# Batch 0 of attention and a maxout network in one kernel: scores before denominators, the first k transposed while q comes, and a new order of loads

## The chip, the cores and the metric

The kernel runs on one core of a Trainium2 chip. The metric is the device time of one execution in microseconds. The engines are named as in the profile: PE (TensorE, the matrix multiplications), DVE (VectorE), ACT (ScalarE), POOL (GpSimd) and SP (SyncE). DMAs are issued by SP, POOL and, twice at the start, by ACT.

## The reference

Eight batches, twelve heads, 448 positions, 64 values per head. Attention with one added to the softmax's denominator, then a maxout network with three first weights and one output weight:

```python
scores = scale * np.matmul(q, k.transpose(0, 1, 3, 2))
m = np.max(scores, axis=-1, keepdims=True)
e = np.exp(scores - m)
attn = e / (np.sum(e, axis=-1, keepdims=True) + np.exp(-m) + 1e-09)
x = np.matmul(attn, v)         # heads side by side: (3584, 768)
h = np.maximum(np.maximum(x @ w1, x @ w2), x @ w3)
out = h @ w_out                # all four weights are 768 x 768
```

The inputs and the output are float32; the kernel multiplies in float16. It leaves the maximum out: exp(s) / (sum of exp(s) + 1) is the same quotient.

## The kernel before

**Tiling.** Two heads make a pair, so a batch has six pairs (`NPAIR`), and pairs are numbered 0 to 47 through all batches. The 448 positions are held as three chunks of 128 and one of 64 (`NB` = 3, `SL` = 64); position 7p + c of a batch stands on partition p in one half of the raw tile. A score tile has keys on partitions and 448 queries along the row, two heads side by side; `scores(p, c)` makes chunk c of pair p, `scores_last(p)` the short chunk of both heads in one matmul. `exp_scores` and `exp_last` are ACT's exponentials. A softmax denominator is a matmul of the exponentials with ones (`den`), the numerator one with v scaled by 256 (`av`, `vst`). ACT computes 1/den as exp(-ln(den + 1)) (`log_one`, `exp_one`), and DVE multiplies it into `xT`, the transposed input of the network (`normalize_one`). In batch 0 denominator and numerator are separate tiles; from batch 1 on one tile holds both (`av_main`, `reciprocals`, `normalize`).

**Loads.** `load(p0, n_pairs, names)` issues, for each of q, k and v, one DMA for the upper and one for the lower half of the partitions, on SP in general. `load_v` does the same for v alone on POOL, and `load_weight(i, half)` loads weight i (0 to 2 are w1 to w3, 3 is w_out), with the cast to float16 done by the DMA, on POOL. There are four sets of raw tiles, each for two pairs (pairs 0 and 1, 2 and 3, and so on, in turn). Pairs of odd batches want zeros in some rows of q, which DVE writes with a memset before the load of the lower half; that DMA waits for it.

**Transposes.** q and k are cast to float16 (`cast_q`, `cast_k`, `cast_k_last`; `cast_qk` does all) and, for pairs 0 to 11 (`P_DMA` = 12), transposed by PE: eight 128 x 128 transposes into one tile in PSUM, which DVE copies to `qkT`. For pair 0 the copy is split between DVE and ACT (lines 243 and 244). From pair 12 on a DMA transposes them. The PSUM pools have two buffers each: `ps_s` for scores, `ps_av` for denominators and numerators, `ps_u` for everything else, the transposes among it, unless `in_scores` puts them into `ps_s`.

**Order.** The order of the instructions of each engine is that of the program, written out by hand (`manual_schedule`). `keep_busy(n)` puts n matmuls of zeros on PE. The loop over `it` from 0 to 11 handles pair `it`:

- `it` 0 makes the scores of pair 0 and the first ones of pair 1. `it` 1 to 4 make the rest of the scores of pair `it`, the denominators and numerators of the pair before, and the transposes and first scores of the pair after.
- `it` 5 ends batch 0: it finishes pairs 4 and 5, transposes pair 6, and starts the network on batch 0 with three tiles of the first weight (`up`), the first four of whose six contraction chunks need pairs 0 to 3 only.
- `batch_done(b)` then puts the rest of that batch's network into a queue, 18 `up` groups of six matmuls (six for each of w1, w2, w3) and six or eight `op` groups (the output weight, 384 columns each). `group()` takes one from the queue. `it` 6 to 11 take three groups each between the steps of attention; the first `op` group comes in `it` 11.
- After the loop, pairs 12 to 47 go two at a time through a second loop, which takes eight to ten groups in each round and ends with what is left in the queue.

**What orders the loads.** SP and POOL issue strictly in program order, and an issue that waits holds up all behind it. SP's loads at `it` 3, 5 and 6 stand behind the memsets of line 498, and POOL's weights behind the scalings of v (`scale_v`), since these are on POOL too. The first half of weight 0 waits in addition for a memset of one column (line 535), which serves as a gate. The weights 1, 2 and 3 follow at `it` 5, 6 and 8; POOL reaches them at 24.71, 26.63 and 30.24 us, as it is far ahead of PE.

Of the kernel before, what the change touches and what calls it, by code (L numbers as in the profile page):

```python
# [21 lines left out]
def kernel(  # L22
# [83 lines left out]
    def load_v(p0, n_pairs):  # L106
        load(p0, n_pairs, "v", (nc.gpsimd, nc.gpsimd))
# [51 lines left out]
        )  # L159

    def cast_qk(p):
        if p == 0:

            qt, kt, _ = raw[0]
            nc.scalar.copy(
                out=k16[0][:, 0:NB], in_=kt[:, 0:2, 0:NB].rearrange("p h c d -> p c h d")
            )
            for eng, cs in ((nc.scalar.copy, slice(0, 2)), (nc.vector.tensor_copy, slice(2, NB + 1))):
                eng(out=q16[0][:, cs], in_=qt[:, 0:2, cs].rearrange("p h c d -> p c h d"))
            cast_k_last(0, nc.gpsimd)  # L170
        else:
            cast_q(p)
            cast_k(p)

    def cast_q(p):
        qt = raw[(p // HB) % NRAW][0]
# [8 lines left out]
        else:  # L185
            nc.vector.tensor_copy(out=q6, in_=qt[:, hs].rearrange("p h c d -> p c h d"))  # L186

    def cast_k(p):
        kt = raw[(p // HB) % NRAW][1]
        hs = slice(2 * (p % HB), 2 * (p % HB) + 2)  # L190
        nc.vector.tensor_copy(  # L191
            out=k16[p % NK][:, 0:NB], in_=kt[:, hs, 0:NB].rearrange("p h c d -> p c h d")
        )
        cast_k_last(p, nc.vector)

    def cast_k_last(p, eng):
        kt = raw[(p // HB) % NRAW][1]
# [16 lines left out]
    def transposes(p, in_scores=False):  # L214
        odd = (p // NPAIR) % 2
        qkT = att_pool.tile([2 * D, 1024], MMDT, tag="qkT", bufs=3)
        qkTs[p] = qkT, 0, S
        if p >= P_DMA:
            nc.sync.dma_start_transpose(
                out=qkT.rearrange("q (c p) -> q c p", p=128),  # L220
                in_=qk16[p % NK].rearrange("p c h d -> p (c h d)"),
            )
            qkTs[p] = qkT, 64 * odd, 512
            return
        if in_scores:
            trT = ps_s.tile([128, 2, 1024], MMDT, tag="s", name="trT")[:, 0]
        else:
            trT = ps_u.tile([128, 1024], MMDT, tag="u", name="trT")


        order = (NB, 0, 1, 2) if odd else (0, 1, 2, NB)
        n0 = 0
        for c in order:
            nc.tensor.transpose(
                out=trT[:, n0 : n0 + 128], in_=q16[p % NK][:, c], identity=ident16
            )
            n0 += SL if c == NB else 128
        for c in range(NB + 1):
            nc.tensor.transpose(
                out=trT[:, S + c * 128 : S + c * 128 + 128], in_=k16[p % NK][:, c], identity=ident16  # L240
            )
        if p == 0:
            nc.vector.tensor_copy(out=qkT[:, 0 : S + 128], in_=trT[:, 0 : S + 128])
            nc.scalar.copy(out=qkT[:, S + 128 : S + 512], in_=trT[:, S + 128 : S + 512])
        else:
            nc.vector.tensor_copy(out=qkT[:, 0 : S + 512], in_=trT[:, 0 : S + 512])  # L246

    def scores(p, c):
        qkT, q0, k0 = qkTs[p]
# [226 lines left out]
    def group():  # L476
        if queue:
            queue.pop(0)()

    LEFT = 4  # L480
    waiting = None
    keep_busy(13)
    cast_qk(0)
    load_v(0, 1)
    transposes(0)
    keep_busy(3)
    for it in range(P_DMA):
# [3 lines left out]
        n_groups = -(-max(len(queue) - LEFT, 0) // to_next) if it % NPAIR else 4  # L491
        n_groups = max(3, min(5, n_groups))

        if it in (3, 5, 6):
            p_new = {3: 7, 5: 8, 6: 9}[it]
            n = p_new // HB % NRAW
            hs = slice(2 * (p_new % HB), 2 * (p_new % HB) + 2)
            nc.vector.memset(raw[n][0][64:128, hs, NB - 1 : NB + 1, :], 0.0)
            if it == 3:
                load(NPAIR, 2, "v")  # L500
                load(p_new, 1, "qk")
            else:
                load(p_new, 1)
        if it == 4:
            load_weight(0, 1)
        if it in (5, 6, 8):
            load_weight((5, 6, 8).index(it) + 1)
        if it < NPAIR:


            if it == 0:
                cast_qk(1)
                scale_v(0)
                load_v(1, 1)
                load_v(2, 2)
                exp_scores(0, 0, scores(0, 0))
                exp_scores(0, 1, scores(0, 1))
                keep_busy(2)
                exp_scores(0, 2, scores(0, 2))
                transposes(1)  # L520
                exp_last(0, scores_last(0))
                keep_busy(2)
                exp_scores(1, 0, scores(1, 0))
            else:
                last = it == NPAIR - 1
                if last:
                    normalize_one(*waiting)
                else:
                    cast_qk(it + 1)
                scale_v(it)  # L530
                if it == 1:
                    load_v(4, 2)
                if it == 3:

                    nc.vector.memset(w_sb[0][:, 0, 0:1], 0.0)
                    load_weight(0, 0)
                if waiting is not None and not last:
                    normalize_one(*waiting)
                exp_scores(p, 1, scores(p, 1))
                den, av = (ps_av.tile([128, 512], FP32, tag="av", name=n) for n in ("den", "av"))  # L540
                sums_main(prev, den, 1)
                stp = scores(p, 2)
                if not last:
                    transposes(it + 1)
                stl = scores_last(p)
                sums_last(prev, den, 1)
                exp_scores(p, 2, stp)
                exp_last(p, stl)
                lnd = log_one(den)
                if not last:  # L550
                    exp_scores(it + 1, 0, scores(it + 1, 0))
                    waiting = prev, av, exp_one(lnd)
                sums_main(prev, av, 0)
                sums_last(prev, av, 0)
            if it == NPAIR - 1:


                den5 = ps_s.tile([128, 2, 512], FP32, tag="s", name="den5")[:, 0]
                sums_main(p, den5, 1)
                sums_last(p, den5, 1)  # L560
                lnd5 = log_one(den5)
                av5 = ps_av.tile([128, 512], FP32, tag="av", name="av")
                sums_main(p, av5, 0)
                sums_last(p, av5, 0)
                rb, rb5 = exp_one(lnd), exp_one(lnd5)
                cast_qk(it + 1)
                normalize_one(prev, av, rb)
                normalize_one(p, av5, rb5)

                ups = [up_open(), up_open(), up_open(ps_av, "av")]  # L570
                for fc, ps in enumerate(ups):
                    up_part(ps, 0, 0, fc, range(4))
                transposes(it + 1, in_scores=True)
                for dc in (4, 5):
                    for fc, ps in enumerate(ups):
                        up_part(ps, 0, 0, fc, (dc,))
                        if dc == 5:
                            up_close(ps, 0, 0, fc)
                batch_done(0)
                del queue[0:3]  # L580
        elif it == NPAIR:
            exp_scores(p, 0, scores(p, 0))
            exp_scores(p, 1, scores(p, 1))
            group()
            cast_qk(it + 1)
            scale_v(it)
            exp_scores(p, 2, scores(p, 2))
            exp_last(p, scores_last(p))
            group()
            transposes(it + 1)  # L590
            group()
        else:
            late = it + 1 < P_DMA
            if not late:

                cast_qk(it + 2)
                transposes(it + 2)
                scale_v(it + 1)
                load(it + 5, 2)
            for c in range(2):  # L600
                exp_scores(p, c, scores(p, c))
            group()
            if late:
                cast_qk(it + 1)
            scale_v(it)
            avs = [av_main(prev, hh) for hh in range(2)]
            av_last(prev, avs)
            stp = scores(p, 2)
            stl = scores_last(p)
            rb = reciprocals(prev, avs)  # L610
            exp_scores(p, 2, stp)
            exp_last(p, stl)
            if late:
                transposes(it + 1)
            group()
            normalize(prev, 0, avs, rb)
            group()
            normalize(prev, 1, avs, rb)
            if it + 2 == P_DMA:
                cast_qk(it + 2)  # L620
                transposes(it + 2)
            for _ in range(n_groups - 3):
                group()
# [7 lines left out]

    avs = [av_main(P_DMA - 1, hh) for hh in range(2)]
    for p in range(P_DMA, NP, 2):
        more = p + 2 < NP
        left = max(len(queue) - LEFT, 0)
# [84 lines left out]
```

## Time and profile before

| | us |
|---|---|
| median of 3 runs | 364.43 (363.88 to 364.97) |
| the profiled execution | 364.45 |
| its span | 362.7 |
| PE busy | 352.6 (97%) |
| DVE, ACT, POOL busy | 244.6, 219.0, 59.1 |
| first scores on PE | 7.34 |
| first `up` on PE | 31.48 |
| first `op` on PE | 68.70 |
| last load of the first 16 pairs issued | 64.77 |

The chain that ended last is 82% PE and 12% DMA, and all of its DMA parts lie in front: loads of v, the first weight, q and k. The DMA engines are over nine tenths busy in nearly all of the slices up to 72 us. A page's busy time counts a matmul from its start to its modelled end, and neighbours overlap, so PE's share is no measure of how much is left; the times between starts are.

### The profile page before, as it was taken

Reading aid. Unit: us, or ns where it says so; the run is one execution under the profiler, and the core shown is the slowest. Engines: PE = TensorE matmul, PEld = TensorE weight load, DVE = VectorE, ACT = ScalarE, POOL = GpSimd, SP = SyncE. Lnnn points to the kernel's source line nnn. Section 1 sums busy time; section 2 is a strip of 40 time slices with the busy share of each in tenths; the row PEclk is TensorE's granted clock in tenths of the full one; section 3 lists DMA queues with packets and bytes.
Section 4 is the critical chain, followed back from the end, with each engine's and each line's share of the span. In section 5 each row is a group of like instructions: output and inputs, shape, how many; then the busy total and the mean of one; then the engine's idle time right before and its main releaser. Section 6 shows DMA issues by size and latency. Waiting matters only on the chain.

```text
span 362.7 us, 5892 instructions
## 1 busy us (share of the span) xinstructions
PE 352.6 (97%) x2072; PEld 165.8 (46%) x2072; DVE 244.6 (67%) x524; ACT 219.0 (60%) x317; POOL 59.1 (16%) x167
## 2 busy tenths in 40 slices
PE   8999998999999999999999999999999999999994
PEld 3334443444444444454444544444444544445552
DVE  4665676866768767767768768668658768646553
ACT  4994576666566765776676666667565767660000
POOL 5673011312011211111021121121121121000000
PEclk9999999999999999999999999999999999999999
DMA  6999999899583994689483995678665961104006
GB/s 174 229 232 238 219 234 242 176 218 247 114 182 89 299 208 105 136 190 228 112 193 71 259 226 112 153 171 232 149 150 78 234 195 29 29 13 120 0 2 174
DMA packets 84942, 58.59 MB, mean 162 GB/s; under 512 B 41680, under 2 KB 81136, under 8 KB 84912
## 3 DMA queue, kind: packets, MB, share of 16 engines
q1 hardware_dynamic: 80144, 51.79, 60.5%
q0 software_dynamic: 4400, 6.10, 9.1%
q10 hardware_dynamic: 368, 0.33, 0.4%
q8 instruction: 16, 0.26, 0.3%
q14 instruction: 14, 0.11, 0.1%
HBM read 42.47 MB, written 11.01 MB: 147 GB/s over the span
## 4 chain that ended last, share of the span: by engine, by line
PE 82%; DMA 12%; POOL 2%; DVE 2%; issue 1%; ACT 0%; POOLq 0%; DVEq 0%
PE up L389 43%; PE op L423 14%; PE av L303 12%; PE stp L252 7%; DMA kin<-in_k_dram 4%; PE av L315 3%; DMA w<-in_moe_w_dram 3%; DMA vin<-in_v_dram 3%; PE stl L282 2%; DMA qin<-in_q_dram 2%; DVE o_sb L448 1%; POOL vin L92 1%; DVE hT L403 0%; DVE xT L337 0%; POOL vst L157 0%
## 5 line engine op out<-in xcount | busy, mean ns | idle before, releaser
L389 PE MATMUL up<-xT,w 128*128 128x448 f16 x864 | 175.2, 353 | 0.9 <-DMA w<-in_moe_w_dram 0.4
L262 ACT ACTIVATE eT<-stp 128x896 f16<-128x896 f32 x144 | 124.4, 911 | 24.5 <-PE stp L252 24.3
L389 PEld LDWEIGHTS <-w 128*128 128x128 f16 x864 | 80.4, 98 | 87.6 <-issue 17.0
L405 DVE TENSOR_TENSOR hT<-hT,up 128x448 f16<-128x448 f16 x96 | 59.1, 621 | 44.2 <-PE up L389 43.5
L157 POOL TENSOR_SCALAR vst<-vin 128x384 f16<-128x384 f32 x132 | 43.6, 341 | 246.9 <-PE av L303 135.6
L328 ACT ACTIVATE lnd<-av 64x448 f32<-64x448 f32 x84 | 45.2, 538 | 62.5 <-PE av L315 61.5
L423 PE MATMUL op<-w,hT 128*128 128x384 f16 x336 | 59.2, 326 | 0.0
L303 PE MATMUL av<-eT,vst 128*128 128x448 f16 x252 | 54.7, 352 | 0.6 <-DVE xT L337 0.6
L337 DVE TENSOR_TENSOR xT<-av,rb 64x448 f16<-64x448 f32 x84 | 52.0, 619 | 1.7
L403 DVE CAST hT<-up 128x448 f16<-128x448 f32 x48 | 29.1, 621 | 25.2 <-PE up L389 24.7
L448 DVE TENSOR_SCALAR o_sb<-op 128x384 f32<-128x384 f32 (+1 forms) x56 | 30.3, 551 | 21.0 <-PE op L423 20.2
L423 PEld LDWEIGHTS <-hT 128*128 128x128 f16 x336 | 31.4, 98 | 26.3 <-issue 5.3
L252 PE MATMUL stp<-qkT 64*128 64x448 f16 x288 | 41.4, 352 | 1.8 <-DVE qkT L246 1.4
L303 PEld LDWEIGHTS <-vst 128*128 128x128 f16 x252 | 24.6, 98 | 23.4 <-DVE xT L337 1.0
L191 DVE CAST qk<-kin 128x384 f16<-128x384 f32 x47 | 25.7, 547 | 2.3 <-DMA kin<-in_k_dram 2.1
L292 ACT ACTIVATE eL<-stl 128x896 f16<-128x896 f32 x18 | 16.5, 917 | 14.2 <-PE stl L282 14.2
L329 ACT ACTIVATE rb<-lnd 128x448 f32<-128x448 f32 x42 | 24.2, 576 | 1.4
L252 PEld LDWEIGHTS <-qkT 64*128 64x128 f16 x288 | 12.6, 94 | 20.1 <-issue 11.9
L199 DVE CAST qk<-kin 64x64 f16<-64x64 f32 x94 | 20.7, 221 | 1.2
L452 ACT ACTIVATE o_sb<-op 128x192 f32<-128x192 f32 x1 | 0.3, 331 | 31.3 <-DVE o_sb L448 31.3
L315 PE MATMUL av<-eL,vst 64*128 64x448 f16 x84 | 15.2, 360 | 0.0
L186 DVE CAST qk<-qin 128x512 f16<-128x512 f32 x29 | 13.2, 455 | 0.2
(54 smaller groups left out, 126.5 us busy)
## 6 DMA issues: line engine op xcount, KB each, us to landing
out_dram<-o_sb SPq DMA_DIRECT2D x54, 192.0 KB, 3.9
qin<-in_q_dram SPq DMA_DIRECT2D x20, 256.0 KB, 3.7
vin<-in_v_dram SPq DMA_DIRECT2D x20, 256.0 KB, 5.3
kin<-in_k_dram SPq DMA_DIRECT2D x19, 256.0 KB, 4.6
qin<-in_q_dram SPq DMA_DIRECT2D x20, 192.0 KB, 3.8
vin<-in_v_dram SPq DMA_DIRECT2D x20, 192.0 KB, 5.3
kin<-in_k_dram SPq DMA_DIRECT2D x19, 192.0 KB, 4.8
w<-in_moe_w_dram POOLq DMA_DIRECT2D x2, 1152.0 KB, 20.1
```

Source lines behind the costliest of these rows:

```text
L157: nc.gpsimd.tensor_scalar(out=out, in0=in_, scalar1=LAMBDA, scalar2=1.0, op0=ALU.mult, op1=ALU.mult)
L252: nc.tensor.matmul(out=stp[:, hh, 0:S], lhsT=qkT[hh * D : hh * D + D, k0 + c * 128 : k0 + c * 128 + 128], rhs=qkT[hh * D : hh * D + D, q0 ...
L262: nc.scalar.activation(out=eT[:, p % 3, c], in_=stp[:, :, 0:S], func=AF.Exp, scale=scale)
L303: nc.tensor.matmul(out=av[:, 0:S], lhsT=vst[:, p % VB, hh * NB + c, (1 - hh) * D : (3 - hh) * D], rhs=eT[:, p % 3, c, hh, :], start=(c == ...
L315: nc.tensor.matmul(out=avs[hh][:, 0:S], lhsT=vst[half, p % VB, 2 * NB, (1 - hh) * D : (3 - hh) * D], rhs=eL[half, p % 2, :], start=False, ...
L328: nc.scalar.activation(out=lnd[mine], in_=avs[hh][other, 0:S], func=AF.Ln, bias=1.0)
L337: nc.vector.tensor_tensor(out=xTs[b][mine, j, :], in0=avs[hh][mine, 0:S], in1=rb[mine], op=ALU.mult)
L389: nc.tensor.matmul(out=ps[:, 0:S], lhsT=w_sb[i][:, dc, ts(fc, 128)], rhs=xTs[b][:, dc, :], start=(dc == 0), stop=(dc == NDC - 1),)
L403: nc.vector.tensor_copy(out=h, in_=ps[:, 0:S])
L405: nc.vector.tensor_tensor(out=h, in0=h, in1=ps[:, 0:S], op=ALU.max)
L423: nc.tensor.matmul(out=ps[:, 0:NW], lhsT=hTs[sb][:, fc, ts(t, 128)], rhs=wout_sb[:, fc, ts(nh, NW)], start=(fc == 0), stop=(fc == NFC - 1),)
L448: nc.vector.tensor_scalar(out=o_sb[:, cs], in0=src, scalar1=1.0 / LAMBDA, scalar2=None, op0=ALU.mult)
```

## The change

- **Pair 0.** k is cast, transposed and copied first, into a score buffer; two zero matmuls follow; then q is cast, transposed into a second tile and copied. Both copies are DVE's, ACT's share of the copy is gone. Ahead of it `keep_busy(13)` becomes `keep_busy(8)`.
- **Pair 1.** The last rows of k are cast by POOL instead of DVE.
- **`it` 1 to 5.** Chunk 2's scores move in front of the denominators of the pair before; the short chunk's exponential is issued directly behind its matmul.
- **End of batch 0.** ACT's ln and exp for the last two pairs are interleaved.
- **v.** Pairs 2 and 3 get a load of their own each (pair 3's at `it` 1) instead of one for both.
- **Pairs 6, 7, 8.** v of pairs 6 and 7 and q and k of pair 7 move from `it` 3 to `it` 4, pair 8 from the start of `it` 5 to behind the normalization of pair 5, each with its memset (now `cleared(p)`). Pair 9 stays at `it` 6.
- **w_out.** It moves from `it` 8 to `it` 9, and waits for a memset of one column there.
- **Pair 7** is transposed in a score buffer.
- **Pair 11.** One group from the queue stands between its two numerators.

```diff
     def cast_qk(p):
-        if p == 0:
-            ...
-        else:
-            cast_q(p)
-            cast_k(p)
+        cast_q(p)
+        cast_k(p, nc.gpsimd if p == 1 else nc.vector)
+    def cast_k0():
+        nc.scalar.copy(
+            out=k16[0][:, 0:NB], in_=raw[0][1][:, 0:2, 0:NB].rearrange("p h c d -> p c h d")
+        )
+        cast_k_last(0, nc.gpsimd)
+    def cast_q0():
+        for eng, cs in ((nc.scalar.copy, slice(0, 2)), (nc.vector.tensor_copy, slice(2, NB + 1))):
+            eng(out=q16[0][:, cs], in_=raw[0][0][:, 0:2, cs].rearrange("p h c d -> p c h d"))
...
+        if p == 0:
+            trK = ps_s.tile([128, 2, 1024], MMDT, tag="s", name="trT")[:, 0]
+            for c in range(NB + 1):
+                nc.tensor.transpose(out=trK[:, ts(c, 128)], in_=k16[0][:, c], identity=ident16)
+            nc.vector.tensor_copy(out=qkT[:, S : S + 512], in_=trK[:, 0:512])
+            keep_busy(2)
+            cast_q0()
+            trQ = ps_u.tile([128, 1024], MMDT, tag="u", name="trT")
+            for c in range(NB + 1):
+                nc.tensor.transpose(out=trQ[:, ts(c, 128)], in_=q16[0][:, c], identity=ident16)
+            nc.vector.tensor_copy(out=qkT[:, 0:S], in_=trQ[:, 0:S])
+            return
...
+    def cleared(p):
+        hs = slice(2 * (p % HB), 2 * (p % HB) + 2)
+        nc.vector.memset(raw[p // HB % NRAW][0][64:128, hs, NB - 1 : NB + 1, :], 0.0)
...
-    keep_busy(13)
-    cast_qk(0)
+    keep_busy(8)
+    cast_k0()
     load_v(0, 1)
     transposes(0)
...
-        if it in (3, 5, 6):
-            ...
-            if it == 3:
+        if it in (4, 6):
+            cleared(7 if it == 4 else 9)
+            if it == 4:
                 load(NPAIR, 2, "v")
-                load(p_new, 1, "qk")
+                load(7, 1, "qk")
             else:
-                load(p_new, 1)
+                load(9, 1)
         if it == 4:
             load_weight(0, 1)
-        if it in (5, 6, 8):
-            load_weight((5, 6, 8).index(it) + 1)
+        if it in (5, 6):
+            load_weight(it - 4)
+        if it == 9:
+            nc.vector.memset(wout_sb[:, 0, 0:1], 0.0)
+            load_weight(3)
...
                 load_v(1, 1)
-                load_v(2, 2)
+                load_v(2, 1)
...
                 if it == 1:
+                    load_v(3, 1)
                     load_v(4, 2)
...
-                exp_scores(p, 1, scores(p, 1))
+                for c in (1, 2):
+                    exp_scores(p, c, scores(p, c))
                 den, av = (ps_av.tile([128, 512], FP32, tag="av", name=n) for n in ("den", "av"))
                 sums_main(prev, den, 1)
-                stp = scores(p, 2)
                 if not last:
                     transposes(it + 1)
-                stl = scores_last(p)
+                exp_last(p, scores_last(p))
                 sums_last(prev, den, 1)
-                exp_scores(p, 2, stp)
-                exp_last(p, stl)
                 lnd = log_one(den)
...
-                lnd5 = log_one(den5)
+                rb = exp_one(lnd)
+                rb5 = exp_one(log_one(den5))
                 ...
-                rb, rb5 = exp_one(lnd), exp_one(lnd5)
                 cast_qk(it + 1)
                 normalize_one(prev, av, rb)
                 normalize_one(p, av5, rb5)
+                cleared(8)
+                load(8, 1)
...
-            transposes(it + 1)
+            transposes(it + 1, in_scores=True)
...
-    avs = [av_main(P_DMA - 1, hh) for hh in range(2)]
+    avs = [av_main(P_DMA - 1, 0)]
+    group()
+    avs.append(av_main(P_DMA - 1, 1))
```

## The prediction

> **What bounds the kernel now.** I read the page first, then stretches of the span, then PE's waits, the places in PE's timeline where they stand, and last the DMA queues. After 90 us PE is all there is; before that it stands still here and there, and the DMA engines are full:
>
> ```profile
> PE 352.6 (97%) x2072; PEld 165.8 (46%) x2072; DVE 244.6 (67%) x524; ACT 219.0 (60%) x317; POOL 59.1 (16%) x167
> ...
> 31.00:60.00 29.00, 27.19 (x176) 12.69 (x175) 18.87 (x41) 17.43 (x27) 2.01 (x7) 1.00 1.15 233
> 60.00:90.00 30.00, 29.40 (x176) 13.37 (x174) 22.24 (x48) 19.12 (x29) 6.27 (x20) 1.00 0.93 217
> 90.00:340.00 250.00, 249.89 (x1434) 118.72 (x1433) 175.62 (x370) 157.16 (x224) 30.30 (x95) 1.00 0.63 148
> ```
>
> From 90 to 340 us PE is busy 249.89 of 250 with code that the change leaves alone, so whatever is won or lost before about 82 us is handed unchanged to the end. From 31 to 60 us the DMA share is 1.15: reordering loads only moves waits about unless it fills a stall. PE's waits between 31 and 90 us, and their places:
>
> ```profile
> PE trT L239 <- DVE qk L191: 1.0, 1, 1.0
> PE av L303 <- DVE xT L337: 0.6, 1, 0.6
> PE up L389 <- DMA w<-in_moe_w_dram: 0.4, 2, 0.2
> PE up L389 <- DVE hT L403: 0.3, 1, 0.3
> ...
> 36.20 1.31 PE L389 MATMUL up<-xT,w 128*128 128x448 f16 x6 [0.21 <-DMA w<-in_moe_w_dram]
> 41.95 1.31 PE L389 MATMUL up<-xT,w 128*128 128x448 f16 x6 [0.18 <-DMA w<-in_moe_w_dram]
> 59.11 0.54 PE L239 MATMUL trT<-ident,qk 128*128 128x128 f16 x4 [1.00 <-DVE qk L191]
> 68.70 1.15 PE L423 MATMUL op<-w,hT 128*128 128x384 f16 x6
> 75.20 0.74 PE L303 MATMUL av<-eT,vst 128*128 128x448 f16 x3 [0.57 <-DVE xT L337]
> ```
>
> "Idle" understates a stall, since the last matmul before it is drawn to its end. By starts: four transposes from 57.73 take 0.22 us, the next stand at 59.11 and come 0.1 us late themselves, so pair 10 lost 1.3 us; three numerator matmuls from 73.90 take 0.57, the next stand at 75.20, so 0.7 us went there. The chain of waits says what PE waits for: the first half of w1, then pair 10's k:
>
> ```profile
> 19.92 11.51 DMA w<-in_moe_w_dram
> 31.48 2.44 PE up L389 x12
> ...
> 43.03 15.35 DMA kin<-in_k_dram
> ```
>
> Three stretches give the DMA prices: 22 to 24.4 us (first pair of lines), 44 to 54 us, 58 to 68 us:
>
> ```profile
> q1 hardware_dynamic: 667, 0.56, 110.9%
> q0 software_dynamic: 3, 0.01, 1.4%
> ...
> q0 software_dynamic: 1000, 1.51, 82.5%
> q1 hardware_dynamic: 1004, 0.81, 31.7%
> ...
> q1 hardware_dynamic: 2784, 2.34, 111.2%
> ```
>
> q0 is POOL's queue, q1 SP's. Both full, they take turns packet by packet: 100 per us each. Alone, SP moves 278 per us, and POOL's full weights 141 (422 packets from 37.5 to 40.5 us). A full weight has 768 packets and 16 for its semaphore: 7.8 us shared, 5.6 alone. The weight issued at 19.92 has no data moving before 24.4: 4.5 us to start.
>
> **The change, part by part.**
>
> *Front.* k is transposed while q is on its way, so four transposes instead of eight follow q's cast at 5.98 us, and the copy behind them has 448 columns instead of 576 (0.46 us; 960 take 0.66, so 0.5 ns each and 0.39). First scores come 0.3 us sooner than 7.34. DVE copies k's half (0.43) before q lands at 5.5, unless that copy is late, which costs its overrun. If the spacing of 0.37 us in the first fillers (13 in 5.03 us) lasts longer now that they are eight, and two after k's transposes, the 0.3 becomes up to -0.4. Pair 1's last k rows move from DVE (0.62 us) to POOL (0.52), in POOL's wait for v (3.00 us idle before 8.74). None of this reaches the end: PE would arrive at its first `up` at 30.9 instead of 31.2, and the weight is not there.
>
> *Two score chunks ahead of the denominators.* Same matmuls between the same ends: the loop from one pair's first scores to the next (17.36, 21.30, 25.23: 3.93 us) is PE's work plus transposes, 0.66 us of copy, first scores. ACT loses a wait of some 0.17 us on chunk 2, but PE's loop doesn't shorten. 0, at most 4 x 0.17 us, and hidden likewise.
>
> *First weight half.* POOL issues it behind pair 3's scaling (19.92). Pair 3's v now has a load of its own, issued in iteration 1 where pairs 4 and 5 were issued (14.71); those needed 7.6 us for 256 KB, and half as much should land at 20 to 20.7. Then 1.0 us of scaling, so issue at 21.0 to 21.8 and data from about 26. SP loses little: pairs 6 and 7's v waits for nothing and goes out at 17.93 as before, only pair 7's second half of q and its k wait for the memset, about 21 instead of 17.4. But pair 8's memset is now behind batch 0's last normalization, at 31.9 instead of 25.28, so SP goes dry near 30 and the weight finishes alone: landing 31.3 against 31.43. Gain 0.15, bounds -0.3 and +0.6. Behind SP's wait stand pair 8's k and v and loads 9 and 10: at the shared rate pair 8's k lands near 38 and pair 9's near 46, cast after 43.8 and 50.2; that cover is four us each.
>
> *Second half and w2.* The second half lands alone near 34 (36.2 before): its wait of 0.3 us goes, and transposing pair 7 in a score buffer takes away the 0.5 us at 39.5. Both only carry PE to the next thing that is late, w2 (issued 24.71, 17.2 us to landing: 41.91). SP's stream is back with data at 33.9, and from there w2 shares: some 45 packets per engine at 16/100 us = 7.2 us, so 41.2 and 0.4 of receipt: 41.6. Gain so far 0.3; bounds 0 and 1.4 (all that PE could have gained).
>
> *Pair 10's k.* After w3 (some 49 us) nothing is in POOL's queue, SP runs alone, and pair 10's k lands near 53 instead of 58.38, five us before its transposes. Gain 1.3.
>
> *w_out.* Before, it was issued at 30.24 and landed 10 us ahead of its first use (68.70). Now POOL issues it behind a DVE memset that follows pair 7's second normalization in iteration 8 (55.57 before). From there to the first `op` are 13.1 us, 11.8 without pair 10's stall. The load needs about 0.1 for the memset, S to start, 7.8 us beside pairs 14 and 15 (still going: SP needs until 60 for load 12, alone), and 0.7 of receipt (issued 30.24 + 27.7 = 57.9; q0 is empty from 57.2). S lies between 2.5 (a v load issued at 9.73 landed whole 3.0 us later) and 4.5 (the weight above). The second is a weight on a full DMA, as here: S = 4.3, in all 12.9, a new wait of 1.1 us; bounds 0 and 1.6. It stands behind nothing else; av of pair 10 and three `op` groups wait behind it. POOL's scaling of pair 9, queued behind the gate, ends near 57.5 and is wanted after 62.
>
> By the Trainium skill, "DMA: Bandwidth & Descriptors", section "Latency and other measured facts", a POOL-issued DMA has its first byte after about 1 us. That would make 9.6 us and no wait; the row at 24.4 speaks against it.
>
> *An `op` group between pair 11's two numerators.* It takes 0.98 us and covers the 0.7 lost at 74.3. But there are two `op` groups left instead of three to hide pair 11's normalization, which ended at 80.06: the first `up` of batch 1 reaches its sixth k chunk some 0.6 us before that. Net +0.3; bounds -0.2 and +0.7.
>
> *Sum*, against the profiled execution's 364.45 us (its span 362.7 and 1.75 around it; the median of the runs is 364.43): 0.3 + 1.3 - 1.1 + 0.3 = 0.8 less, rounded up to 0.9 for ends of S that lie below: 363.5.
>
> **The rivals.**
>
> *No w_out wait.* If data starts within 3.2 us of the issue (4.3 less the wait), all of pair 10's 1.3 stays: 0.3 + 1.3 + 0.3 = 1.9 less, 362.5; with the bound of 1.4 at w2, 361.5. For it: the v load's 3.0 in all. Against: the start at 24.4. The skill's 1 us is this case.
>
> *Slower: the first weight waits for pair 3's v.* Were that load to land as late as pairs 4 and 5's in the profile (23.5), the weight would be issued at 24.6, start at 29.1, run alone for 3 us and land at 32.7. The second half follows at 35.7, w2 then shares from its first packet: 35.7 + 7.8 = 43.5, 1.6 later than 41.91. With the rest of the sum: -1.6 + 1.3 - 1.1 + 0.3 = 1.1 slower, 365.6. It decides once the weight is issued after about 23 us. For it: POOL stands strictly in order, and its queue did take 7.6 us here. Against: half the bytes.
>
> *The loads don't move what PE sees.* SP still issues v of pairs 6 and 7 where it did, and a DMA at 1.15 has as much to move. If pair 10's k stays late because pair 8 and 9's loads are issued 6 us later, its 1.3 us remains and the w_out wait falls away with it; only small gains are left, 364.3.
>
> **How the numbers follow.** Forecast 0.45, no w_out wait 0.33, slower 0.12, nothing moved 0.10. A measurement of this kernel can tell about 0.3% (1.1 us) from no change. Faster than that: the second case, and a third of the first where the wait is under 0.8: 0.47. Slower: most of the third case and a corner of the first: 0.11. Same: 0.42. Range: 361.9 (no wait and some gain at w2) to 364.9 (w_out at its worst, first weight a little late). The likeliest case alone: 362.9 to 364.2.
>
> **What would show it.** In PE's waits the entry of `trT` on `qk` (1.0) gone; `up` on `w` still there, once or twice, at 31 and 41 us; a new entry of `op` on the w_out load near 67 to 68 us; `av` on `xT` replaced by `up` on `xT` near 78 us. In POOL's timeline the first weight between 21.0 and 21.8, w_out near 55.4, landing 12 to 13 us later. In SP's timeline a hole from about 24 to 32 us. I am wrong if `op` doesn't wait, if the first `up` starts after 32 us, or if anything differs in length beyond 90 us.

## The result: slower by 0.7%, and the profile after

The changed kernel takes 367.26 us (median of 15 runs, 364.37 to 368.70); before, beside it, 364.52 us (15 runs, 363.88 to 365.57). The ratio is 1.007, 95% interval [1.0052, 1.0088]: slower by 2.7 us where 0.9 us faster was forecast, and outside the range. The profiled execution took 366.41 us (span 364.6), 1.96 more than the one of before. One execution of e2 (374.84 us, the one that its profile shows) and one of e3 (715.92 us) were slow, and all medians and ratios below leave them out.

Stretches of the span, after; the third column group is PE, and PEclk, DMA share and GB/s end the line:

```profile
31.00:60.00 29.00, 28.74 (x189) 13.58 (x187) 20.55 (x45) 17.46 (x27) 4.10 (x12) 1.00 1.15 234
60.00:90.00 30.00, 26.46 (x150) 12.20 (x149) 19.22 (x43) 17.63 (x27) 4.74 (x15) 0.94 0.88 200
90.00:340.00 250.00, 249.89 (x1434) 118.48 (x1433) 176.09 (x371) 158.28 (x225) 30.82 (x96) 1.00 0.65 151
```

Up to 60 us PE does more than before (28.74 us busy, 27.19 before), and beyond 90 us nothing has changed. All that is lost is lost between 60 and 90 us, and there are two losses in that line: PE is 2.9 us less busy, and its mean granted clock is 0.94, where before showed 1.00. PE's waits and the places in PE's timeline, after:

```profile
PE op L433 <- DMA w<-in_moe_w_out_dram: 2.8, 1, 2.8
PE up L399 <- DVE xT L347: 0.5, 1, 0.5
PE av L313 <- DVE xT L347: 0.2, 1, 0.2
PE up L399 <- DMA w<-in_moe_w_dram: 0.2, 1, 0.2
```

```profile
31.16 2.43 PE L399 MATMUL up<-xT,w 128*128 128x448 f16 x12
41.01 1.31 PE L399 MATMUL up<-xT,w 128*128 128x448 f16 x6 [0.17 <-DMA w<-in_moe_w_dram]
57.01 0.39 PE L253 MATMUL trT<-ident,qk 128*128 128x128 f16 x4
65.95 0.55 PE L262 MATMUL stp<-qkT 64*128 64x448 f16 x4
69.35 2.10 PE L433 MATMUL op<-w,hT 128*128 128x384 f16 x6 [2.85 <-DMA w<-in_moe_w_out_dram]
71.24 1.78 PE L313 MATMUL av<-eT,vst 128*128 128x448 f16 x6
```

Pair 10's transposes (57.01) wait for nothing any more, and w2's first `up` stands at 41.01 instead of 41.95. Both gains reach the first `op`: 2.26 us earlier than the 68.70 of before, PE could have begun it at 66.44. It begins at 69.35. Then look at the second column: six `op` matmuls are drawn with 2.10 us, where the same six took 1.15 before, and six of `av` with 1.78 instead of 1.30. They ran at half the clock, which was granted from 68.80 us for 3.413 us.

The account by starts of the same matmuls, before and after: w2's first `up` 0.95 us earlier; pair 10's first `up` behind its transposes 2.26 earlier (59.49, 57.23); the first `op` 0.65 later (68.70, 69.35), so 2.91 went into the wait; the second `op` group 2.04 later (71.60, 73.64), so 1.39 went into the halved clock; from 87 us on everything 1.96 later, so 0.08 was won in between. That is the 1.96 us of the two profiled executions. The medians lie 2.7 us apart, and the changed kernel's times go with the clock: of its 15 runs, the three with the lowest mean granted clock (0.989 and 0.990) took 368.47 to 368.70 us, the two with the highest (0.997) 364.37 and 366.00, and the profiled one (0.992) is the fastest of the ten between.

Where w_out's time went is in POOL's timeline and in the chain of waits, after:

```profile
23.38 1.75 POOL L147 DMA_DIRECT2D w<-in_moe_w_dram  x2
55.05 0.86 POOL L147 DMA_DIRECT2D w<-in_moe_w_out_dram  x1 [9.37 <-DMA qin<-in_q_dram]
```

```profile
55.05 14.25 DMA w<-in_moe_w_out_dram
69.35 2.10 PE op L433 x6
```

The gate's memset ran at 54.69, POOL issued at 55.05, the first packet moved 3.54 us later, the packets took 10.2 us, and from the last of them to the last report (the receipt) went 0.5. POOL's line names a load of q as what ended its wait; but in e1, e2b, e3 and e4 as well POOL issues w_out 0.36 us behind the start of the memset, so the memset is what it waits for. The first of the sixteen DMA engines reported at 66.50, the last at 69.30. The DMA queues from 58.6 to 66 us, after (packets, MB, share of sixteen engines):

```profile
q0 software_dynamic: 657, 1.01, 74.4%
q1 hardware_dynamic: 862, 0.71, 39.6%
```

POOL's w_out (q0) and SP's loads (q1: the end of load 12, which landed at 61.71, and load 14) share the engines, and SP's smaller packets come somewhat faster.

### The profile page after: what moved, and what is told of

It reads as the page before. It is cut to its first block, busy times and chain, and to the rows that moved or that the text cites. A ratio compares the mean times of both kernels' runs of the same rounds, so it can differ in the third digit from the quotient of the medians.

```text
span 364.6 us, 5892 instructions
## 1 busy us (share of the span) xinstructions
PE 351.2 (96%) x2069; PEld 165.4 (45%) x2069; DVE 244.2 (67%) x524; ACT 218.9 (60%) x316; POOL 60.9 (17%) x171
## 4 chain that ended last, share of the span: by engine, by line
PE 81%; DMA 9%; ACT 5%; DVE 2%; issue 1%; SPq 1%; DVEq 0%
PE up L399 42%; PE op L433 14%; PE av L313 12%; PE stp L262 7%; DMA w<-in_moe_w_out_dram 4%; PE av L325 3%; DMA kin<-in_k_dram 3%; ACT eT L272 3%; DMA qin<-in_q_dram 2%; PE stl L292 2%; DVE o_sb L458 1%; DVE xT L347 1%; ACT rb L380 1%; ACT eL L305 1%; ACT lnd L375 0%
## 5 line engine op out<-in xcount | busy, mean ns | idle before, releaser
L433 PE MATMUL op<-w,hT 128*128 128x384 f16 x336 | 60.1, 330 | 2.8 <-DMA w<-in_moe_w_out_dram 2.8
L262 PE MATMUL stp<-qkT 64*128 64x448 f16 x288 | 40.4, 352 | 2.8 <-DVE qkT L256 1.7
L200 DVE CAST qk<-kin 64x64 f16<-64x64 f32 x92 | 20.7, 225 | 1.2
L187 DVE CAST qk<-qin 128x512 f16<-128x512 f32 x29 | 12.4, 426 | 0.2
```

The costliest lines, as they stand in the source:

```text
L262: nc.tensor.matmul(out=stp[:, hh, 0:S], lhsT=qkT[hh * D : hh * D + D, k0 + c * 128 : k0 + c * 128 + 128], rhs=qkT[hh * D : hh * D + D, q0 ...
L433: nc.tensor.matmul(out=ps[:, 0:NW], lhsT=hTs[sb][:, fc, ts(t, 128)], rhs=wout_sb[:, fc, ts(nh, NW)], start=(fc == 0), stop=(fc == NFC - 1),)
```

## The experiments

Theory: the loss is the wait on w_out, which is issued one iteration too late, and a halved clock that follows a long idle stretch. Rivals: the loss sits in the front or in batch 0's order; the wait isn't w_out's own lateness but comes from the loads beside it; the slow matmuls behind the wait have nothing to do with the idling.

**e1: w_out one iteration earlier.**

```diff
-        if it == 9:
+        if it == 8:
             nc.vector.memset(wout_sb[:, 0, 0:1], 0.0)
             load_weight(3)
```

> The changed kernel with w_out and its gate at iteration 8 instead of 9, the rest unchanged. Theory (w_out lands 2.9 us after its first op, and PE's idling halves its clock behind it): POOL issues w_out near 48.7 us, it lands near 62, before its use at 66.4; its packets now share with pair 10's k, which comes back late by 0.5 to 1.2 us at 56.8. No wait of op, no halved clock: 362.8 to 363.8 us. Rival (the loss lies in something else in front, such as the later loads of pairs 8 and 9): the time stays above 366.

Measured: 362.11 us (361.68 to 362.63), ratio to before 0.9944 [0.9927, 0.9962]. POOL issued w_out at 48.26, it landed at 61.30 and `op` began at 66.01, on time. PE's waits between 31 and 90 us, all of them:

```profile
PE up L399 <- DVE xT L347: 0.5, 1, 0.5
```

One digit turns the change from slower to faster, so the rest of it, taken together, does no harm. It came out below the expected interval, since pair 10's k, which I expected to be delayed by w_out, was not: SP's load 10 got most of its k through before w_out's data moved, and its two halves landed at 52.18 and 52.99.

**e2 and e2b: before, with only w_out moved to iteration 9 behind its memset.**

```diff
-        if it in (5, 6, 8):
-            load_weight((5, 6, 8).index(it) + 1)
+        if it in (5, 6):
+            load_weight(it - 4)
+        if it == 9:
+            nc.vector.memset(wout_sb[:, 0, 0:1], 0.0)
+            load_weight(3)
```

> The kernel before with w_out alone moved to iteration 9 behind a gate. Theory: pair 10's k is no longer late (1.3 us won), op would start at 67.4 us, w_out is issued at 55.7 and lands 13 to 14 us later: a wait of 1.5 to 2.5 us, with the clock halved in part of the executions (another 0 to 1.3 us). 364.5 to 367, slower than before or level. Rival (w_out is harmless without the other parts): 363.2.

> Before with only w_out moved to iteration 9 behind a memset, looked at once more for its profile. Theory: op waits for w_out 2.5 to 3.5 us from about 67.4 us, the clock is halved for 3.4 us behind it (1.3 to 1.7 us lost), pair 10's k lands before 55 and its wait is gone: 366.5 to 368.5. Rival (another place loses the time): the wait on w_out is under 2 us and the clock stays whole.

Measured: e2 367.97 us, ratio 1.0111 [1.0083, 1.0138], above the interval expected; e2b, one more execution of the same kernel, 365.64 us, below its own. So w_out alone makes a slower kernel than the whole change, as it should if the rest of the change brings 0.95 us at w2. In e2b the last matmul ahead of the wait starts at 67.23 and the first `op` at 70.09, when w_out had just landed (70.05), yet the clock stayed at 1.00: I expected the halving in each execution and it is not in each. The mean clocks of e2's five runs, 0.990 to 0.994, suggest that it was in those; no profile shows it.

**e3: pairs 14 and 15 loaded one iteration later,** so that w_out has less beside it.

```diff
-        if it in (8, 9):
-            load({8: 12, 9: 14}[it], 2)
+        if it in (8, 10):
+            load({8: 12, 10: 14}[it], 2)
```

> The changed kernel with the load of pairs 14 and 15 behind pair 12's transpose on SP (iteration 10 instead of 9), so that w_out has the DMA engines nearly to itself. Theory (w_out's landing is set by taking turns with that load): w_out moves at up to 141 packets per us instead of 100 and lands at 65 to 66.5 us, op waits 0 to 0.5 us, no halved clock: 362.2 to 363.0 us. Rival (w_out is late because POOL issues it late, whatever shares the engines): landing near 69 as in the changed kernel, 366 to 367.

Measured: 364.05 us, ratio 0.9996 [0.9980, 1.0012], 1 us above the interval expected. w_out landed 11.6 us after its issue instead of 14.25, and `op` began at 66.98, 0.3 us late. So 2.6 us of w_out's landing time is the company of load 14. A new wait ate part of the gain, as the waits of e3 show:

```profile
PE stl L292 <- DMA qkT<-qk: 1.5, 1, 1.5
```

Pair 13's DMA transpose stands behind load 14 in SP's order; it was issued at 74.76 and landed at 80.63.

**e4: the changed kernel with twelve zero matmuls ahead of the first `op` group,** so that PE does not idle where it waits.

```diff
+            if it == P_DMA - 1:
+                keep_busy(12)
```

> The changed kernel with 12 matmuls of zeros (2.3 us at 0.19 each) ahead of the first op group, in the time in which PE waits for w_out anyway. Theory (the wait of 3.2 us halves PE's clock for 3.4 us, which costs 1.3 us of its own): op starts when it did, near 69.4, the halved stretch behind it is gone: 365.4 to 366.2 us. Rival (the slow matmuls behind the wait have nothing to do with PE's idling): 367.3 as before, or more by fillers that end late.

Measured: 366.07 us (365.17 to 366.38), ratio 1.0046 [1.0028, 1.0064]. All six runs had a mean clock of 0.997 to 1.000, and the timeline of its profile shows `op` at its normal length behind a wait that ended even later (w_out took 15.5 us to land):

```profile
66.30 2.44 PE L392 MATMUL busy<-idle 128*128 128x448 f16 x12
70.45 1.15 PE L433 MATMUL op<-w,hT 128*128 128x384 f16 x6 [1.71 <-DMA w<-in_moe_w_out_dram]
```

Work of no use made the kernel 1.2 us faster than the changed one by the medians, 0.9 by the ratios to the before measured beside each: that is the halved clock, apart from the wait.

**e5: the whole change with w_out issued where it was before.**

```diff
-        if it in (5, 6):
-            load_weight(it - 4)
-        if it == 9:
-            nc.vector.memset(wout_sb[:, 0, 0:1], 0.0)
-            load_weight(3)
+        if it in (5, 6, 8):
+            load_weight((5, 6, 8).index(it) + 1)
```

> The whole change, but w_out issued where it was before (behind w3's group, iteration 8, no memset as gate); everything else as changed. Theory (the loss is the wait of the first op group on w_out, 2.9 us, and the halved clock behind it, 1.3 us): both go; w_out's data then shares the DMA engines with loads 8 to 10 from about 49 us, so pair 10's k lands again near 58 and PE waits 1.3 to 2 us for it; w2's gain of 0.9 and nothing else are left: about 364 us, 363.3 to 364.6, ratio 0.997 to 1.000 of before. Rival A (the loss sits in the front or in the batch 0 order, not in w_out): the time stays at 366 to 367. Rival B (pair 10's k is not delayed by w_out): 362.3 to 362.8.

Measured: 365.59 us (364.05 to 367.31), ratio 1.0031 [1.0012, 1.0051]: 1 us above the interval expected. PE's waits between 30 and 90 us, e5:

```profile
PE trT L253 <- DVE qk L192: 2.1, 2, 1.7
PE up L399 <- DVE xT L347: 0.5, 1, 0.5
PE trT L248 <- DVE qk L187: 0.3, 1, 0.3
PE up L399 <- DMA w<-in_moe_w_dram: 0.2, 1, 0.2
```

The mechanism was right: pair 10's k landed at 58.67 and 59.45, pair 9's was late as well (the other wait on `qk`). What I had not counted is that the twelve runs fall into two groups. Six have a mean clock of 0.997 to 1.000 and took 364.05 to 364.93, as expected; six have 0.994 or 0.995 and took 366.24 to 367.31. The profiled one is of the second group, and its clock halved from 60.44 us on, just when twelve `up` matmuls began that take 2.43 us at full clock:

```profile
60.58 4.05 PE L399 MATMUL up<-xT,w 128*128 128x448 f16 x12
```

The groups lie 2.1 us apart. A halved stretch of 3.413 us can cost 1.7 us at most, so the clock makes most of the difference, and the rest, perhaps a longer wait in those runs, is open: the first group has no profile.

**e6, e7, e8, e9: parts of the change taken away from e1.** All four have w_out in iteration 8.

e6 puts the front back: pair 0's q and k together, 13 fillers, pair 1's last k rows on DVE, and in the loop

```diff
-                for c in (1, 2):
-                    exp_scores(p, c, scores(p, c))
+                exp_scores(p, 1, scores(p, 1))
...
+                stp = scores(p, 2)
...
-                exp_last(p, scores_last(p))
+                stl = scores_last(p)
...
+                exp_scores(p, 2, stp)
+                exp_last(p, stl)
```

> The change with w_out one iteration earlier (the run e1, 362.1 us) and the front as before: pair 0's q and k cast and transposed together, 13 fillers, pair 1's last k rows on DVE, chunk 2's scores behind the denominators. Theory (the front reaches nothing, since the first up waits for PE's own arrival or the first weight, which lie within 0.4 us of each other): the first up starts at 31.2 to 31.5 instead of 31.0 to 31.2, the time is 362.0 to 362.6, at most 0.3 above e1. Rival (the front brings what it saves at the first scores, 0.6 us, or more through the four loops): 362.7 to 363.3.

Measured: 361.86 us, ratio 0.9929 [0.9914, 0.9943]. The first `up` stands at 31.01 (30.97 in e1). The front brings nothing. My reason for that was only half right: in e1 and e6 the weight is there in time, PE is what is late, and still the front's gain doesn't arrive. The new order gives it back in pairs 0 and 1, where chunk 2 waits for ACT's exponentials, which hold the score buffers (`stp` on `eT`, 0.34 and 0.79 us in the changed kernel, no such entry in e6). The second of them, in the changed kernel:

```profile
11.34 0.36 PE L262 MATMUL stp<-qkT 64*128 64x448 f16 x2 [0.79 <-ACT eT L272]
```

e7 puts load 8 back:

```diff
+        if it == 5:
+            cleared(8)
+            load(8, 1)
...
-                cleared(8)
-                load(8, 1)
```

> The change with w_out one iteration earlier (e1, 362.1 us) and load 8 with its clearing back at the start of iteration 5. Theory (w2's earlier landing comes from SP's data coming back late, at 36.5 us instead of 32, because load 8 is issued behind batch 0's last normalization): with load 8 back, w2 lands at 41.3 to 42 instead of 39.7 and PE waits 0.7 to 1.3 us there again: 362.7 to 363.4. Rival (w2's gain comes from its earlier start or from pairs 6 and 7 alone): w2 lands before 40.5 and the time stays within 0.2 of e1.

Measured: 362.94 us, ratio 0.9960 [0.9945, 0.9974]. w2 landed at 41.90, against 41.91 before and 39.72 in e1. Waits between 30 and 90 us, and the longer of the two on a weight, e7:

```profile
PE up L399 <- DMA w<-in_moe_w_dram: 1.2, 2, 0.7
PE up L399 <- DVE xT L347: 0.5, 1, 0.5
...
31.82 2.44 PE L399 MATMUL up<-xT,w 128*128 128x448 f16 x12 [0.74 <-DMA w<-in_moe_w_dram]
```

So w2's gain is load 8's place: in the changed kernel SP issues nothing between 24.3 and 32.6 us, and its data is back only at some 36.5 us, so the first weights have the engines nearly to themselves for longer. That holds for the first weight as well: with load 8 back its first half lands at 31.77 instead of 30.32 (e1), and the first `up` is 0.85 us later.

e8 takes the `op` group between pair 11's numerators away:

```diff
-    avs = [av_main(P_DMA - 1, 0)]
-    group()
-    avs.append(av_main(P_DMA - 1, 1))
+    avs = [av_main(P_DMA - 1, hh) for hh in range(2)]
```

> The change with w_out one iteration earlier (e1, 362.1 us), without the op group between pair 11's two numerators (so it runs one place later, behind the first scores of the next pair). Theory by the prediction's own term (it covers 0.7 us of av's wait on xT and gives 0.4 back as up's wait on xT): 362.3 to 362.5, the wait of av on xT near 0.5 is back and the one of up on xT goes. Rival (the wait only changes place, the loss of 0.66 us at the first up of batch 1 is as large as the one removed): within 0.15 of e1.

Measured: 361.97 us, ratio 0.9934 [0.9919, 0.9949]; its interval overlaps e1's. The wait of `av` on `xT` is back with 0.6, that of `up` on `xT` (0.5) is gone. The rival held: the group moves a wait and removes none.

e9 puts pair 12's and 13's last scores ahead of the third `op` group:

```diff
-        group()
-        exp_last2(scores_last2(p))
+        if p == P_DMA:
+            exp_last2(scores_last2(p))
+            group()
+        else:
+            group()
+            exp_last2(scores_last2(p))
```

> The change with w_out one iteration earlier (e1, 362.1 us), and at the start of batch 1 the last scores of pairs 12 and 13 ahead of the third op group instead of behind it, so that they stand where PE waits for xT. Theory: the gap of 0.66 us ahead of the sixth k chunk of the first up holds only because two op groups are too little to hide pair 11's normalization; the order of these two changes nothing in the work ahead of that up (both stand before it or both behind), so the gain is at most the two matmuls' 0.4 us if they were behind that up before, and 0 if both stood ahead: 361.7 to 362.2. Rival (the exponentials of the last scores, started sooner on ScalarE, delay the relu of the op group): 362.3 to 362.8.

Measured: 361.86 us, ratio 0.9928 [0.9909, 0.9947], no difference from e1 that these runs can tell. The wait of `up` on `xT` is gone from the profile, but 0.33 us (by starts) now stands ahead of the last scores, which wait for ACT.

**e10: before, with only w_out moved to iteration 8 behind its memset** (e2 with `if it == 8`).

> Before with only w_out moved: issued in iteration 8 behind a memset (48 us), all else as before. Theory (of e1's gain of 2.3 us, pair 10's k is 1.3 and the rest, 0.9, is w2's earlier landing, which load 8's place brings): the wait of pair 10's transposes is gone, w2 still lands near 41.9, w_out lands near 62 to 64, ahead of its first use at 67.4; 363.0 to 363.5, ratio 0.996 to 0.9975. Rival (w_out alone delays pair 10's or 12's loads, since it shares with them from 52 us): a wait of 0.5 us or more on qk or on w_out comes back, 363.6 to 364.6.

Measured: 363.08 us (362.91 to 363.50), ratio 0.9960 [0.9946, 0.9974]. Waits between 31 and 90 us, e10:

```profile
PE av L303 <- DVE xT L337: 0.6, 1, 0.6
PE up L389 <- DMA w<-in_moe_w_dram: 0.3, 1, 0.3
PE up L389 <- DVE hT L403: 0.3, 1, 0.3
```

No wait on `qk`, none on w_out. This is the smallest edit tried that is faster, 1.4 us; load 8's place adds 0.8 to 1.0 by the medians and 0.6 by the ratios (e1 against e10 and against e7), and front and `op` group add nothing that was measured. e7 and e10 have the same ratio, 0.9960, and differ by all that the change does beside w_out and load 8: the parts that no run undoes by itself (the loads of v, the interleaved ln and exp, loads 6 and 7, pair 7's score buffer) add nothing together with front and `op` group either. The versions with both (e1, e6, e8, e9; 361.9 to 362.1 us) beat both kernels; e6 and e8 are the simpler ones.

## Why the prediction was wrong, step by step

- **The w_out wait, 1.1 us with bounds 0 and 1.6: the failed term.** Measured 2.91 us. From the gate to the moment PE wanted the weight were 11.75 us, against 11.8 in the sum; that side was right. The load took 14.6 from the gate, against 12.9. Its pieces, with those of the sum in brackets: gate to issue 0.36 (0.1), start 3.54 (S = 4.3), packets 10.2 (7.8), receipt 0.5 (0.7). S, which I bounded from 2.5 to 4.5, was not the problem. The 7.8 was: 784 packets at 100 per us. By the queue rows above, q0 got 89 per us while all its engines were at work (657 packets in 7.4 us), which makes 8.8 us; and a mean rate says when the mean engine is done, while the semaphore needs the last of sixteen, here 2.8 us behind the first. The trace of before showed this spread, in the same weight: its first engine reported at 55.36, its last at 57.94. I took the landing of a whole load as data plus receipt and gave this term no bound of its own.
- **The halved clock: 1.39 us, in no term.** The forecast wait of 1.1 us would hardly have brought it, since before's wait of 1.0 us for pair 10's k left the clock whole; that of 2.9 us did. That a long enough wait costs more than its length was missing even from the bounds, so the range's upper end, "w_out at its worst", stood 1.4 us above the forecast where the runs stand 3.8 above.
- **Pair 10's k, 1.3 us: right.** Measured 1.31; k landed at 53.40 and 54.21, forecast near 53.
- **w2, 0.3 us with bounds 0 and 1.4:** 0.95, inside the bounds. SP was issuing again at 32.6, but its data moved only from about 36.5 us, not from 33.9, and shared less of w2's time; landing 40.96 against 41.6. e7 shows that load 8's place does it.
- **First weight half, 0.15 us:** the step was wrong and harmless. Pair 3's v landed at 21.28 and 22.24, not at 20 to 20.7, and POOL issued the weight at 23.38 instead of 21.0 to 21.8. That is past the point from which the rival "slower" was to decide, but the weight landed at 30.80, 1.9 us ahead of that rival's 32.7: its data started 2.2 us behind the issue, not 4.5. The rival's sign came true by another mechanism.
- **Front and score chunks, nothing:** right in outcome. First scores came 0.6 us sooner (6.76) and the loops took 3.83 instead of 3.93 us; e6 shows that none of it reaches the first `up`.
- **The `op` group between the numerators, 0.3 us:** 0.08 by the account above, inside its bounds of -0.2 to 0.7; e8 measured none.
- **Sights:** the waits of `op` on w_out and of `up` on `xT` came as foretold, `trT`'s wait on `qk` went, and SP's hole is there; 0.2 us of `av` on `xT` stayed, and nothing differs beyond 90 us. The sum had the right list of terms for loads and the wrong size for one of them.

The Trainium skill's rival, a first byte about 1 us after a POOL issue ("DMA: Bandwidth & Descriptors", "Latency and other measured facts"), did not hold on these full queues: the trace shows 3.54 us for w_out.

## What to carry to other kernels

When a load is moved to "just in time", reckon with the landing of its slowest DMA engine, from a landing of the same load in the trace, and leave a margin of several us: here 11.8 us of lead met 14.6 us of need, and one iteration more of lead made the same change 0.6% faster than before instead of 0.7% slower. A stall of PE can cost half as much again through the clock (1.4 us behind 2.9 here), in some executions of a program and not in others. Undo the parts of a change one by one: of the many here, two carried all that was measured, one of them with the wrong sign.

## What the runs showed of the hardware

**The clock is judged in fixed stretches of 3.413 us.** The granted clock of the changed kernel was halved from 68.80 us for 3.413 us, that of e5 from 60.44 us for 3.413 us, and in both the time at full clock before it is a whole number of such stretches (64.85 = 19 x 3.413 and 54.61 = 16 x 3.413). So it is in the other traces at full clock, up to the halving at the end of the kernel: 351.57, 354.99 and 358.40 us are 103, 104 and 105 of them. Here is the stretch just before each of the two halvings, after and e5, and the emptiest such stretch of e2b ahead of the kernel's end, behind which the clock was not halved. Behind the stretch and its length in us, the first number is PE's busy time; the third from the end is the granted clock inside the stretch:

```profile
65.39:68.81 3.42, 1.11 (x8) 0.21 (x5) 3.29 (x9) 2.13 (x3) 0.00 (x0) 1.00 1.11 259
```

```profile
57.03:60.44 3.41, 1.47 (x13) 0.57 (x12) 1.26 (x4) 2.89 (x5) 0.00 (x0) 1.00 1.13 240
```

```profile
65.90:69.31 3.41, 1.67 (x11) 0.51 (x8) 3.25 (x7) 2.69 (x4) 0.00 (x0) 1.00 0.95 224
```

PE busy 1.11 or 1.47 us of such a stretch: the next one runs at half the clock. PE busy 1.67 us: it does not. e2b's wait (2.6 us) is nearly as long as that of the changed kernel (2.9), but only 1.8 us of it lie in this stretch, against 2.4 in the changed kernel. This would explain why one program gives two groups of times (e5) and why the changed kernel's runs spread over 4 us where before spreads over 1.7: where the stretches' borders fall differs between executions. The other traces at full clock agree: no stretch with 1.67 us or more is followed by a halved one (1.90 in e3, 2.41 before), and each with 1.47 or less is, the last ones of the kernels included (1.28 in e8, 1.07 in the changed kernel). Where the border lies between 1.47 and 1.67 was not tried by itself. The Trainium skill, "TensorE: Matmul & The Clock Gate", Part 1, has a free-running window of 3413 ns, and the trace agrees with its 3.413 us. The same page of the Trainium skill, in the table of "Why this matters for your kernels", warns of idle gaps over some 3 us between bursts of matmuls; in e5 the idle was in two pieces with four transposes between them, the longer of them 1.89 us from start to start, so the limit is lower here than the page's.

**A weight's sixteen engines finish up to 2.9 us apart** on full queues: 2.9 in e4, 2.8 in the changed kernel, 2.6 before and in e1, 1.9 in e7 and e9; where less moved beside it, in e3, 1.6. From issue to landing the same load, with no other weight ahead of it, took from 11.6 us (e3) to 15.5 us (e4). e3 has less beside it; but e4 and the changed kernel (14.25) issue the same loads beside it, so over 1 us of it differs between executions.
